# Expert stage: the second product's accumulators put two to a PSUM bank, four banks in rotation

## Chip, core and metric

One core of a Trainium2 chip runs the whole program. Its engines are TensorE (PE in the rows; PEld is its weight load), VectorE (DVE), ScalarE (ACT), GpSimd (POOL) and SyncE (SP, which issues most DMAs). The metric is the device time of one execution, in microseconds (us). PSUM, in which TensorE accumulates, has eight banks of 512 float32 columns over 128 partitions; this kernel uses all eight in the stage that is changed.

## What is computed

Three layers, one after the other. An FFT convolution over 8 x 3072 tokens of 256 features gives `x`. Then a mixture of eight experts, of which each token goes to one; then a dense two-product layer. The change is in the experts:

```
for e in range(E):                     # E = 8, FF = 1024, D = 256
    mask = e_idx == e                  # e_idx = argmax(x @ w_gate)
    ...
    h = np.maximum(x[mask] @ w1[e], 0.0)
    ye = h @ w2[e]
    out[mask] = gate_w[mask, None] * eom[mask, e, None] * ye
```

## The kernel before

The 24,576 tokens are grouped by expert into blocks: 41 blocks of 512 tokens and up to 21 of 256 tokens for what is left over (17 of them were executed). `experts(ids, first)` walks through the blocks; from the twelfth place on, a 256-token block stands after every two 512-token blocks. Each block takes eight ticks, one for each 128 of the 1024 hidden features. Numbers are split in a high and a low part (`hh` and `hl`, `w2h` and `w2l`), so each product is three matmuls: high with high, high with low, low with high.

A tick `t` records, in this order, which is also the order in which each engine executes (the schedule is written out by hand):

- TensorE: `gemm1` (L586), six matmuls of the first product into a bank of the pool `ph` (four banks).
- ScalarE: the relu (L867), which writes `hh`; then VectorE: the low part `hl` (L868).
- ScalarE and VectorE: one eighth of the next block's weights is split (`split_w`, L633 and L634). SyncE loads the weights of the block after that: `w1r` is issued in the fourth tick, `w2r` in the last (L613, L618), each 1 MB.
- TensorE: `gemm2` (L595) of the tick two before this one, into the block's accumulators `pz`. The accumulators collect over the block's eight ticks.
- Only after a block's last `gemm2`: ScalarE copies the accumulators out to `zo` (L896), and SyncE stores `zo` to HBM (L898).

A 512-token block has four accumulators of 128 tokens x 256 features, a 256-token block has two. Each has a bank of its own, of which it uses half. The four banks are named:

```
pz[j2] = pz_tiles(nt, 0 if nt == 4 or j2 % 2 else 2)
```

A 512-token block takes banks 0 to 3, a 256-token block 0 and 1 or 2 and 3 in turn. So the first `gemm2` of the next block goes into a bank that the block before has just finished with, and it must wait for that bank's copy. The two ticks between `gemm1` and `gemm2` mean that TensorE has one more `gemm1` to do after a block's last `gemm2`, before it comes to that wait.

The second layer (L923 on) has accumulators of the same kind (L1087, evicted at L1096) that already stand two to a bank.

Of the kernel before, what the change touches and what calls it, by code (L numbers as in the profile page):

```python
# [9 lines left out]
F32 = mybir.dt.float32  # L10
# [6 lines left out]
PSUM = bass.MemoryType.PSUM  # L17
# [3 lines left out]
NB, SEQ, D = 8, 3072, 256  # L21
# [105 lines left out]
def fftconv_moe_moe2(ctx: ExitStack, tc: tile.TileContext, x, ffl, fny, wg, w1, w2, win, wout,  # L127
                     t_sq, t_m2, t_m3, t_sg, t_sm, out):
    nc = tc.nc
    V, S, G, T = nc.vector, nc.scalar, nc.gpsimd, nc.tensor  # L130
# [145 lines left out]
    pools = {}  # L276
# [111 lines left out]
    def scatter(m, after=None):  # L388

        for i in range(min(m, len(scat))):  # L390
            b, n, pos, tid = scat.pop(0)
            if after is not None:
                G.tensor_copy(gap, after)
            else:
                G.memset(gap, 0.0)
            i = G.indirect_dma_start(
                out=xid, out_offset=bass.IndirectOffsetOnAxis(ap=pos[:, n:n + 1].bitcast(U32), axis=0),
                in_=tid[:, n:n + 1], in_offset=None)
            tc.declare_no_dep(i.ins, group="scatter", reason="every token has a row of its own")
            tc.add_to_no_dep_group("scatter", i.ins)  # L400
            if b >= BE:
                tc.declare_no_dep(i.ins, group="early", reason="the first blocks hold tokens of earlier batches")
                tc.add_to_no_dep_group("late", i.ins)
# [143 lines left out]
    pzs = ctx.enter_context(ExitStack())  # L547
# [32 lines left out]
    def gemm1(wh, wl, xh, xl, f, w):  # L580
        p = pools["ph"].tile([128, 512], F32, name="ph", tag="ph")
        n = 0
        for k in range(2):
            ws = slice(128 * f, 128 * f + 128)
            for a, b in ((wh, xh), (wh, xl), (wl, xh)):
                T.matmul(p[:, 0:w], a[:, k, ws], b[:, k, 0:w], start=n == 0, stop=n == 5)  # L586
                n += 1
        return p

    def gemm2(hh, hl, wh, wl, f, last, pz):  # L590
        for c, z in enumerate(pz):
            ts = slice(128 * c, 128 * c + 128)
            n = 0
            for a, b in ((hh, wh), (hh, wl), (hl, wh)):
                T.matmul(z, a[:, ts], b[:, f, :], start=f == 0 and n == 0, stop=f == last and n == 2)  # L595
                n += 1

    def pz_tiles(nt, first):
        return [pools["pz"].tile([128, 512], F32, name="pz", tag=f"pz{first + c}")[:, 0:D] for c in range(nt)]

    raw, wt, xg, xt = {}, {}, {}, {}

    def nt_of(j):
        return 4 if j < NFULL else 2

    def load_w(j, which):
        if j is None:
            return
        if which == 0:
            e = nc.sync.value_load(eidx[0:1, j:j + 1], min_val=0, max_val=E - 1)  # L610
            raw[j] = [e, None, None]
            t = pools["raw"].tile([128, 2, FF], F32, name="w1r")
            nc.sync.dma_start(t, w1[bass.ds(e, 1)].rearrange("o (c p) f -> p (o c) f", p=128))  # L613
            raw[j][1] = t
        else:
            e = raw[j][0]
            t = pools["raw"].tile([128, 8, D], F32, name="w2r")
            nc.sync.dma_start(t, w2[bass.ds(e, 1)].rearrange("o (c p) f -> p (o c) f", p=128))  # L618
            raw[j][2] = t

    def split_w(j, i):
        if j is None:
            return
        if i == 0:
            wt[j] = [pools["we"].tile([128, 2, FF], F32R, name="w1h"), pools["we"].tile([128, 2, FF], F32R, name="w1l"),
                     pools["we"].tile([128, 8, D], F32R, name="w2h"), pools["we"].tile([128, 8, D], F32R, name="w2l")]
        if i < 4:
            at = (slice(None), i // 2, slice(512 * (i % 2), 512 * (i % 2) + 512))
            src, h, l = raw[j][1][at], wt[j][0][at], wt[j][1][at]
        else:  # L630
            at = (slice(None), slice(2 * (i - 4), 2 * (i - 4) + 2), slice(None))
            src, h, l = raw[j][2][at], wt[j][2][at], wt[j][3][at]
        S.copy(h, src)  # L633
        V.tensor_tensor(l, src, h.bitcast(F32), op=ALU.subtract)  # L634
# [6 lines left out]
    def load_tok(j):  # L641
        if j is None:
            return
        nt = nt_of(j)
        assert j < NE or not (scat or gating)
        G.memset(gap, 0.0)
        ids = pools["m"].tile([128, 4], I32, name="ids")
        if nt == 4:
            i = G.indirect_dma_start(
                out=ids, out_offset=None, in_=xid.rearrange("(a c) o -> a (c o)", c=4),  # L650
                in_offset=bass.IndirectOffsetOnAxis(ap=xidx[:, j:j + 1].bitcast(U32), axis=0))
            early(j, i)
        else:
            for c in range(2):
                o = NFULL + 2 * (j - NFULL) + c
                G.indirect_dma_start(
                    out=ids[:, c:c + 1], out_offset=None, in_=xid,
                    in_offset=bass.IndirectOffsetOnAxis(ap=xidx[:, o:o + 1].bitcast(U32), axis=0))
        t = pools["m"].tile([128, 4, D], F32, name="xg")
        for c in range(nt):  # L660
            i = G.indirect_dma_start(  # L661
                out=t[:, c, :], out_offset=None, in_=yn if j >= NE else yn[0:BE * SEQ, :],
                in_offset=bass.IndirectOffsetOnAxis(ap=ids[:, c:c + 1].bitcast(U32), axis=0))
            early(j, i)
        xg[j] = t
# [130 lines left out]
    for k in range(ng * NB + 4 + nu):  # L796
        b, i = divmod(k, ng)
# [42 lines left out]
    load_w(1, 0)  # L840
    load_w(1, 1)
    latep.close()
    pools["pz"] = pzs.enter_context(tc.tile_pool(name="pzp", bufs=1, space=PSUM, side="right", reuse_waits="tile"))
    gating.append(gate(NB - 1, pools["ph"], "ph"))
    gating.append(tables())
    def clear():
# [7 lines left out]
    def experts(ids, first):  # L854
        ex = None
        hq, pz = {}, {}
        ns = 8 * len(ids)
        ids = ids + [None, None]
        for t in range(ns + 2):
            n, f = divmod(t, 8)  # L860
            j, ja, jb = (ids + [None])[n:n + 3]
            if t < ns:
                w = 128 * nt_of(j)
                p = gemm1(wt[j][0], wt[j][1], *xt[j], f, w)
                hh = pools["m"].tile([128, 512], F32R, name="hh", bufs=3)
                hl = pools["m"].tile([128, 512], F32R, name="hl", bufs=3)
                S.activation(hh[:, 0:w], p[:, 0:w], AF.Relu)  # L867
                V.scalar_tensor_tensor(hl[:, 0:w], p[:, 0:w], 0.0, hh[:, 0:w].bitcast(F32),  # L868
                                       op0=ALU.max, op1=ALU.subtract)
                hq[t] = hh, hl  # L870
                split_w(ja, f)
                if f == 3:
                    load_w(jb, 0)
                if f == 7:
                    load_w(jb, 1)
                if f == 4:
                    load_tok(jb)
                scatter(1, tick(hh[:, 0:1].bitcast(F32)))
                go_on(1)
                if first and ex is None and not gating and not scat:  # L880
                    open_layer_pools()
                    clear()
                    ex = extra()
                if ex is not None and j < NFULL:
                    next(ex, None)
            if t >= 2:
                j2, f2 = ids[(t - 2) // 8], (t - 2) % 8
                nt = nt_of(j2)
                if f2 == 0:
                    pz[j2] = pz_tiles(nt, 0 if nt == 4 or j2 % 2 else 2)  # L890
                hh, hl = hq.pop(t - 2)
                gemm2(hh, hl, wt[j2][2], wt[j2][3], f2, 7, pz[j2])
                if f2 == 7:
                    zo = pools["m"].tile([128, 4, D], F32, name="zo")
                    for c, z in enumerate(pz.pop(j2)):
                        S.copy(zo[:, c, :], z)  # L896
                    r0 = 512 * j2 if nt == 4 else ZREM + 256 * (j2 - NFULL)
                    nc.sync.dma_start(zs[r0:r0 + 128 * nt, :].rearrange("(p c) d -> p c d", c=nt), zo[:, 0:nt, :])  # L898
                    wt.pop(j2)
                    xt.pop(j2)  # L900
            if t < ns and f in (5, 6):
                prep_x(ja, f - 5)
# [23 lines left out]
    with ExitStack() as c3:  # L926
# [112 lines left out]
        hq, zq, zo, cc = {}, {}, {}, {}  # L1039
# [4 lines left out]
        def bank():  # L1044
            return pools["ph"].tile([128, 512], F32, name="ph", tag="ph")
# [79 lines left out]
        for t in range(npair + 1):  # L1125
# [17 lines left out]
            if j == 0:  # L1143
                ws = wsums(q)
                for n, u in enumerate(PLAIN):
# [3 lines left out]
                    b = bank()  # L1149
# [97 lines left out]
```

## Time and profile before

| | |
|---|---|
| time, median of 3 runs | 3904.09 us (3898.43 to 3909.12) |
| the profiled execution | 3879.73 us, its span 3878.0 us |
| TensorE busy | 3786.5 us, 98% of the span |
| VectorE, ScalarE, GpSimd busy | 70%, 61%, 26% |
| expert stage | from about 560 to 1760 us of the span |
| ScalarE's copies of 256 columns (L896) | 198, mean 387 ns |
| second layer's copies of 512 columns (L1096) | 96, mean 594 ns |

A row of a timeline gives the start and the duration in us, the engine, the line of the kernel, the operation, what it writes and reads, and in square brackets how long the engine had been idle and who ended that. A duration of a matmul is longer than its distance to the next one, since matmuls are pipelined. The granted clock is the share of TensorE's full clock: 1.00 is 2.4 GHz and 0.50 is 1.2 GHz.

### The profile page before, as it was taken

Reading aid. Unit: us, or ns where it says so; the run is one execution under the profiler, and the core shown is the slowest. Engines: PE = TensorE matmul, PEld = TensorE weight load, DVE = VectorE, ACT = ScalarE, POOL = GpSimd, SP = SyncE. Lnnn points to the kernel's source line nnn. Section 1 sums busy time; section 2 is a strip of 40 time slices with the busy share of each in tenths; the row PEclk is TensorE's granted clock in tenths of the full one; section 3 lists DMA queues with packets and bytes.
Section 4 is the critical chain, followed back from the end, with each engine's and each line's share of the span. In section 5 each row is a group of like instructions: output and inputs, shape, how many; then the busy total and the mean of one; then the engine's idle time right before and its main releaser. Section 6 shows DMA issues by size and latency. Waiting matters only on the chain.

```text
span 3878.0 us, 63612 instructions
## 1 busy us (share of the span) xinstructions
PE 3786.5 (98%) x24340; PEld 3378.1 (87%) x24340; DVE 2716.8 (70%) x4910; ACT 2378.2 (61%) x4573; POOL 1010.4 (26%) x1159
## 2 busy tenths in 40 slices
PE   6999999999999999998999999999999999999999
PEld 3777778898889899997899999999999999999998
DVE  4667766577878755555777777777777777777776
ACT  3777764455454555554666666666666666666666
POOL 3044556422222222215222111112222111112200
PEclk8999999999999999999999999999999999999999
DMA  9666543445555444440000000000000000000000
GB/s 253 207 204 200 171 147 121 145 137 173 167 164 163 161 159 148 154 138 28 28 25 25 34 22 23 23 23 27 23 26 25 33 23 23 23 23 27 24 17 22
DMA packets 195396, 345.09 MB, mean 89 GB/s; under 512 B 26320, under 2 KB 112464, under 8 KB 194704
## 3 DMA queue, kind: packets, MB, share of 16 engines
q1 hardware_dynamic: 167376, 289.60, 22.9%
q0 software_dynamic: 27296, 51.36, 4.8%
q8 instruction: 192, 3.15, 0.3%
q14 instruction: 116, 0.95, 0.1%
q10 hardware_dynamic: 416, 0.03, 0.0%
HBM read 238.31 MB, written 102.60 MB: 88 GB/s over the span
## 4 chain that ended last, share of the span: by engine, by line
PE 47%; ACT 4%; DVE 2%; issue 1%; POOL 0%; DMA 0%; ACTq 0%; POOLq 0%; DVEq 0%
PE pz L1087 23%; PE ph L1029 21%; ACT sig L1053 1%; PE ph L1035 1%; ACT zo L1096 1%; PE pt L958 1%; ACT sp L1066 1%; DVE cc L1204 1%; DVE xl L965 0%; ACT xh L964 0%; DVE cc L1193 0%; DVE rw L1001 0%; DVE hl L1062 0%; ACT hh L1058 0%; POOL zg L942 0%
## 5 line engine op out<-in xcount | busy, mean ns | idle before, releaser
L1087 PE MATMUL pz<-wouth,hh 128*128 128x256 f32 x3072 | 873.0, 284 | 0.0
L1087 PE MATMUL pz<-wouth,hl 128*128 128x256 f32 x3072 | 868.7, 283 | 0.0
L1087 PE MATMUL pz<-woutl,hh 128*128 128x256 f32 x3072 | 868.2, 283 | 0.0
L1062 DVE TENSOR_TENSOR hl<-cc,hh 128x512 fp32r<-128x512 f32 x768 | 523.3, 705 | 155.0 <-ACT hh L1058 154.3
L1087 PEld LDWEIGHTS pz<-wouth,hh 128*128 128x128 f32 x3072 | 585.3, 191 | 30.0
L1087 PEld LDWEIGHTS pz<-woutl,hh 128*128 128x128 f32 x3072 | 586.0, 191 | 26.8
L942 POOL DMA_INDIRECT zg<-zs,posz x192 | 213.2, 1111 | 1515.0 <-PE pt L958 1358.2
L1087 PEld LDWEIGHTS pz<-wouth,hl 128*128 128x128 f32 x3072 | 585.5, 191 | 0.3 <-DVE hl L1062 0.3
L867 ACT ACTIVATE hh<-ph 128x512 fp32r<-128x512 f32 (+1 forms) x464 | 249.0, 537 | 527.3 <-PE ph L586 440.4
L1066 ACT COPY sp<-ph 128x512 f32<-128x512 f32 x552 | 324.1, 587 | 381.4 <-PE ph L1029 380.4
L868 DVE SCALAR_TENSOR_TENSOR hl<-ph,hh 128x512 fp32r<-128x512 f32 (+1 forms) x464 | 283.6, 611 | 333.9 <-ACT hh L867 314.4
L1058 ACT CAST hh<-cc 128x512 fp32r<-128x512 f32 x768 | 476.1, 620 | 34.8 <-DVE cc L1161 33.0
L595 PE MATMUL pz<-w2h,hh 128*128 128x256 f32 x1584 | 447.9, 283 | 24.6 <-ACT zo L896 24.4
L595 PE MATMUL pz<-w2h,hl 128*128 128x256 f32 x1584 | 445.6, 281 | 0.0
L595 PE MATMUL pz<-w2l,hh 128*128 128x256 f32 x1584 | 445.2, 281 | 0.0
L1053 ACT ACTIVATE sig<-cc 128x512 f32<-128x512 f32 x552 | 349.4, 633 | 133.1 <-DVE cc L1204 67.9
L661 POOL DMA_INDIRECT xg<-yn,ids x198 | 199.5, 1008 | 758.7 <-PE ph L571 663.9
L586 PE MATMUL ph<-xh,w1h 128*128 128x512 f32 (+1 forms) x928 | 348.7, 376 | 4.1 <-issue 4.1
L586 PE MATMUL ph<-xl,w1h 128*128 128x512 f32 (+1 forms) x928 | 339.0, 365 | 0.3 <-DVE xl L577 0.2
L595 PEld LDWEIGHTS pz<-w2h,hh 128*128 128x128 f32 x1584 | 300.6, 190 | 43.5 <-ACT zo L896 29.2
L586 PE MATMUL ph<-xh,w1l 128*128 128x512 f32 (+1 forms) x928 | 335.7, 362 | 0.0
L595 PEld LDWEIGHTS pz<-w2l,hh 128*128 128x128 f32 x1584 | 302.1, 191 | 12.7
(240 smaller groups left out, 8280.6 us busy)
## 6 DMA issues: line engine op xcount, KB each, us to landing
w1r<-in_w_dram SPq DMA_DIRECT2D x58, 1024.0 KB
w2r<-in_w_dram SPq DMA_DIRECT2D x58, 1024.0 KB
us<-u SPq DMA_DIRECT2D x96, 256.0 KB
u<-us SPq DMA_DIRECT2D x128, 192.0 KB
out_dram<-zo SPq DMA_DIRECT2D x46, 512.0 KB
yn<-yt SPq DMA_DIRECT2D x90, 256.0 KB
xt<-in_x_dram SPq DMA_DIRECT2D x84, 256.0 KB
zs<-zo SPq DMA_DIRECT2D x41, 512.0 KB
```

Of the source, the lines that this page charges most:

```text
L586: T.matmul(p[:, 0:w], a[:, k, ws], b[:, k, 0:w], start=n == 0, stop=n == 5)
L595: T.matmul(z, a[:, ts], b[:, f, :], start=f == 0 and n == 0, stop=f == last and n == 2)
L661: i = G.indirect_dma_start(out=t[:, c, :], out_offset=None, in_=yn if j >= NE else yn[0:BE * SEQ, :], in_offset=bass.IndirectOffsetOnAxis( ...
L867: S.activation(hh[:, 0:w], p[:, 0:w], AF.Relu)
L868: V.scalar_tensor_tensor(hl[:, 0:w], p[:, 0:w], 0.0, hh[:, 0:w].bitcast(F32), op0=ALU.max, op1=ALU.subtract)
L942: G.indirect_dma_start(out=t[:, c, :], out_offset=None, in_=zs, in_offset=bass.IndirectOffsetOnAxis(ap=posz[0][:, o:o + 1].bitcast(U32), a ...
L1029: T.matmul(out, w, x, start=start and n == 0, stop=n == 2, skip_group_check=True)
L1053: S.activation(t, src, AF.Sigmoid, scale=1.702)
L1058: S.copy(hq[t, u][0], cc[u])
L1062: V.tensor_tensor(l, cc[u], h.bitcast(F32), op=ALU.subtract)
L1066: S.copy(t, x)
L1087: T.matmul(z[:, 256 * (c % 2):256 * (c % 2) + 256], a[:, ts], wm[w][:, 2 * q + i, :], start=first and m == 0, stop=m == 2, skip_group_chec ...
```

## The change

The accumulators become tiles of 2 x 256 columns, so that two share a bank: a 512-token block has two tiles, a 256-token block one. All tiles have one tag in a pool of four buffers, so the four banks are taken in turn, whatever the block's size. Only the first matmul into a bank carries the flag `start` (f = 0, first half); the second half's first matmul goes without it. A copy takes the whole bank, 512 columns.

```diff
-    def gemm2(hh, hl, wh, wl, f, last, pz):
-        for c, z in enumerate(pz):
-            ts = slice(128 * c, 128 * c + 128)
-            n = 0
-            for a, b in ((hh, wh), (hh, wl), (hl, wh)):
-                T.matmul(z, a[:, ts], b[:, f, :], start=f == 0 and n == 0, stop=f == last and n == 2)
-                n += 1
-
-    def pz_tiles(nt, first):
-        return [pools["pz"].tile([128, 512], F32, name="pz", tag=f"pz{first + c}")[:, 0:D] for c in range(nt)]
+    def gemm2(hh, hl, wh, wl, f, pz):
+
+        for b, z in enumerate(pz):
+            for c in range(2):
+                ts = slice(256 * b + 128 * c, 256 * b + 128 * c + 128)
+                for n, (a, w) in enumerate(((hh, wh), (hh, wl), (hl, wh))):
+                    T.matmul(z[:, c, :], a[:, ts], w[:, f, :], start=f == 0 and c == 0 and n == 0, stop=n == 2,
+                             skip_group_check=True)
+
+    def pz_tiles(nt):
+        return [pools["pz"].tile([128, 2, D], F32, name="pz", tag="pz") for _ in range(nt // 2)]
...
-    pools["pz"] = pzs.enter_context(tc.tile_pool(name="pzp", bufs=1, space=PSUM, side="right", reuse_waits="tile"))
+    pools["pz"] = pzs.enter_context(tc.tile_pool(name="pzp", bufs=4, space=PSUM, side="right", reuse_waits="tile"))
...
-                    pz[j2] = pz_tiles(nt, 0 if nt == 4 or j2 % 2 else 2)
+                    pz[j2] = pz_tiles(nt)
...
-                gemm2(hh, hl, wt[j2][2], wt[j2][3], f2, 7, pz[j2])
+                gemm2(hh, hl, wt[j2][2], wt[j2][3], f2, pz[j2])
...
-                        S.copy(zo[:, c, :], z)
+                        S.copy(zo[:, 2 * c:2 * c + 2, :], z)
```

No engine's instructions come in another order; what changes is the banks, the waits and the copies. TensorE at the first `gemm2` tick of the second block, before, with the engines that a row waits for in brackets (`Activation` is ScalarE):

```order
L595 MATMUL pz<-w2h,hh 128x256 [waits Activation_49]
L595 MATMUL pz<-w2l,hh 128x256
L595 MATMUL pz<-w2h,hl 128x256 [waits DVE_49]
L595 MATMUL pz<-w2h,hh 128x256 [waits Activation_49]
L595 MATMUL pz<-w2l,hh 128x256
L595 MATMUL pz<-w2h,hl 128x256
L595 MATMUL pz<-w2h,hh 128x256 [waits Activation_49]
L595 MATMUL pz<-w2l,hh 128x256
L595 MATMUL pz<-w2h,hl 128x256
```

The same nine places in the changed kernel, whose `gemm2` matmuls have line 596:

```order
L596 MATMUL pz<-w2h,hh 128x256 [waits Activation_49]
L596 MATMUL pz<-w2l,hh 128x256
L596 MATMUL pz<-w2h,hl 128x256 [waits DVE_49]
L596 MATMUL pz<-w2h,hh 128x256
L596 MATMUL pz<-w2l,hh 128x256
L596 MATMUL pz<-w2h,hl 128x256
L596 MATMUL pz<-w2h,hh 128x256
L596 MATMUL pz<-w2l,hh 128x256
L596 MATMUL pz<-w2h,hl 128x256
```

Before, each accumulator's first matmul waits for a copy of the block before; after, the one wait for ScalarE that is left is the one for this tick's `hh`. ScalarE at the end of a 512-token block, before:

```order
L867 ACTIVATE hh<-ph 128x512
L633 CAST w1h<-w1r 128x512
L896 COPY zo<-pz 128x256 x4
L867 ACTIVATE hh<-ph 128x512
L633 CAST w1h<-w1r 128x512
```

And at the same place in the changed kernel, where the relu is L868, the cast L634 and the copy L897:

```order
L868 ACTIVATE hh<-ph 128x512
L634 CAST w1h<-w1r 128x512
L897 COPY zo<-pz 128x512 x2
L868 ACTIVATE hh<-ph 128x512
L634 CAST w1h<-w1r 128x512
```

Four copies became two at the same place; on both sides they stand behind the relu and the weight cast of the next block's second tick.

## Rows read from the trace of the kernel before

**Rows 1.** The profile's page: the span, and each engine's busy time.

```profile
span 3878.0 us, 63612 instructions
PE 3786.5 (98%) x24340; PEld 3378.1 (87%) x24340; DVE 2716.8 (70%) x4910; ACT 2378.2 (61%) x4573; POOL 1010.4 (26%) x1159
```

**Rows 2.** Waits of TensorE in the expert stage (total, times, longest), and the page's group.

```profile
PE pz L595 <- ACT zo L896: 24.4, 13, 3.0
...
L595 PE MATMUL pz<-w2h,hh 128*128 128x256 f32 x1584 | 447.9, 283 | 24.6 <-ACT zo L896 24.4
```

**Rows 3.** Stretches: busy time by engine, granted clock, DMA share, GB/s.

```profile
1340.00:1700.00 360.00, 360.00 (x2492) 333.90 (x2491) 209.52 (x359) 187.72 (x392) 93.18 (x103) 1.00 0.47 154
2000.00:3800.00 1800.00, 1794.54 (x11722) 1633.21 (x11721) 1327.45 (x2046) 1197.60 (x2129) 362.27 (x320) 1.00 0.08 25
```

**Rows 4.** Timeline of one wait, where a 256-token block follows a 512-token block.

```profile
893.76 0.39 SPq L618 DMA_DIRECT2D w2r<-in_w_dram  x1
...
895.54 0.28 PE L586 MATMUL ph<-xh,w1l 128*128 128x256 f32 x1
...
897.68 0.28 PE L586 MATMUL ph<-xh,w1l 128*128 128x256 f32 x1
898.31 0.38 ACT L867 ACTIVATE hh<-ph 128x256 fp32r<-128x256 f32 x1 [3.69 <-PE ph L586]
...
898.73 0.42 DVE L868 SCALAR_TENSOR_TENSOR hl<-ph,hh 128x256 fp32r<-128x256 f32 x1 [2.94 <-ACT hh L867]
899.10 1.20 ACT L896 COPY zo<-pz 128x256 f32<-128x256 f32 x4
...
900.07 0.39 PE L595 MATMUL pz<-w2h,hh 128*128 128x256 f32 x1 [2.12 <-ACT zo L896]
...
900.62 0.42 DVE L868 SCALAR_TENSOR_TENSOR hl<-ph,hh 128x256 fp32r<-128x256 f32 x1 [0.69 <-ACT hh L867]
...
901.84 0.28 PE L595 MATMUL pz<-w2h,hl 128*128 128x256 f32 x1
...
903.26 0.28 PE L595 MATMUL pz<-w2h,hl 128*128 128x256 f32 x1
```

**Rows 5.** The stretch of that wait: busy time by engine, granted clock, DMA share, GB/s.

```profile
896.00:899.00 3.00, 1.96 (x17) 1.75 (x15) 0.27 (x1) 0.69 (x2) 1.56 (x2) 1.00 1.03 352
```

**Rows 6.** Timeline of TensorE: four of the thirteen waits.

```profile
593.36 0.39 PE L595 MATMUL pz<-w2h,hh 128*128 128x256 f32 x1 [1.47 <-ACT zo L896]
...
644.27 0.58 PE L595 MATMUL pz<-w2h,hh 128*128 128x256 f32 x1 [3.03 <-ACT zo L896]
...
1263.54 0.39 PE L595 MATMUL pz<-w2h,hh 128*128 128x256 f32 x1 [2.11 <-ACT zo L896]
...
1325.10 0.39 PE L595 MATMUL pz<-w2h,hh 128*128 128x256 f32 x1 [1.55 <-ACT zo L896]
```

**Rows 7.** TensorE alone in the five half-clock stretches: busy time, clock, DMA.

```profile
643.47:650.29 6.82, 6.02 (x22) 0.50 0.21 79
...
1264.69:1268.11 3.42, 3.42 (x18) 0.50 0.35 144
sum 20.48, PE 19.68; mean PE 3.94
```

**Rows 8.** ScalarE's copies out of accumulators by shape: busy, mean ns, idle before.

```profile
L896 ACT COPY zo<-pz 128x256 f32<-128x256 f32 x198 | 61.2, 387 | 5.5 <-PE ph L586 3.0 <-PE pz L595 2.4
...
L1096 ACT COPY zo<-pz 128x512 f32<-128x512 f32 x96 | 49.4, 594 | 3.7 <-PE pz L1087 3.3
```

**Rows 9.** Timeline: first and last of twelve accumulating matmuls, expert stage and second layer.

```profile
895.66 0.28 PE L595 MATMUL pz<-w2h,hh 128*128 128x256 f32 x1
...
896.96 0.28 PE L595 MATMUL pz<-w2h,hl 128*128 128x256 f32 x1
...
2406.90 0.28 PE L1087 MATMUL pz<-wouth,hh 128*128 128x256 f32 x1
...
2408.21 0.28 PE L1087 MATMUL pz<-wouth,hl 128*128 128x256 f32 x1
```

## The prediction

> **What bounds the kernel now.** I read the page first. TensorE is busy for 3786.5 of 3878.0 us [rows 1], so an edit in the expert stage can only gain what TensorE idles there, or what makes it slow there. The second view is therefore the waits of TensorE between 560 and 1760 us. One row holds nearly all: 24.4 us in 13 waits, the longest 3.0 us, of `gemm2` for ScalarE's copies out of `pz`; the page has the same sum on the first of the three matmuls of a `gemm2` [rows 2]. In a stretch of the stage after the last of these waits, TensorE works 360.00 of 360.00 us at full clock [rows 3]: no second limit shows behind TensorE, neither in ScalarE (188 us of 360) nor in VectorE (210).
>
> The third view is the timeline around one wait [rows 4], a 512-token block followed by one of 256. `gemm1` of the new block's second tick ends at 895.54 + 0.28 = 895.82. Its relu starts only at 898.31, 2.5 us late, and the copies stand behind that relu and a weight cast in ScalarE's order, so they start at 899.10. TensorE has meanwhile done one more `gemm1`, is through at 897.68 + 0.28 = 897.96, and stands for 2.12 us until the copy of its bank is done. The reader should see two things: ScalarE is late, not slow (it was idle for 3.69 us before that relu), and the copies pass this lateness on to TensorE. In those 3 us the DMA engines are fully occupied, share 1.03 at 352 GB/s [rows 5], by the 1 MB of `w2r` issued at 893.76 [rows 4]. That the load delays the signal from TensorE to ScalarE is a guess of mine; the change leaves it as it is.
>
> The fourth view is the granted clock. Five waits are followed by a stretch at 0.50, 1.2 GHz: the one that ends at 644.27 by 643.47 to 650.29, the one that ends at 1263.54 by 1264.69 to 1268.11 [rows 6, 7]. The five last 20.48 us together, with 19.68 us of TensorE work [rows 7]. Between 1340 and 1700 us, where there is no wait, the clock stays at 1.00 [rows 3].
>
> **The change part by part.** *The waits for the copies go.* A block's accumulators now lie in banks that the block before does not use; the last user of a bank is four tiles back, at least one whole 512-token block. The built order shows this: the waits for a copy at the first `gemm2` tick are gone, and the wait left on that tick's first matmul is for its own relu. Gain: 24.4 us [rows 2].
>
> *Half-clock stretches go with them.* Work of 19.68 us at 1.2 GHz is 9.84 us of work at 2.4 GHz, so 19.68 - 9.84 = 9.8 us come back if all five are due to the waits [rows 7]. From below it is nothing, if the clock falls there anyway; I take the whole, because the clock is at 1.00 in the 360 us without a wait.
>
> *What is late next.* The late relu stays, so its next reader is TensorE's `gemm2` of the same tick. In the timeline the low part `hl` of that tick is ready at 898.73 + 0.42 = 899.15, and the matmul that reads it runs at 901.84. Without the wait it would run 2.12 us earlier, at 899.72: still 0.57 us of slack. The following tick is tighter, since its relu stands behind the copies: `hl` is ready at 900.62 + 0.42 = 901.04, and its reader moves from 903.26 to 901.14. That leaves 0.10 us [rows 4]. So the cover is just enough at its tightest place. If it is missed by as much as it now holds, each of 13 places loses some 0.1 us, 1.3 us in all; I take 1 us. If the cover did not exist at all, the wait would only move from the copy to the relu, and 24.4 us would be the price.
>
> *Copies of 512 columns.* Four copies of 256 take 1.20 us together [rows 4]; two of 512, at 594 ns each by the second layer's [rows 8], take 1.19 us end to end and less where they overlap, as the four do (4 x 387 ns would be 1.55). The relu behind them is not later than now. At the stage's end the last block's copy is one of 594 instead of two of 387, of which the first overlaps matmuls: it lands about 594 - 387 = 0.2 us later, once, on the path to the second layer. VectorE, GpSimd and the DMA queues keep their instructions and order; their cover is TensorE, which stays the longest.
>
> *Two accumulators in one bank.* The order of matmuls stays; only the address changes. Twelve matmuls of the expert stage start 896.96 - 895.66 = 1.30 us apart, 118.2 ns from one to the next; twelve of the second layer, whose accumulators already share banks, 2408.21 - 2406.90 = 1.31 us, 119.1 ns [rows 9]. The 3 x 1584 = 4752 matmuls [rows 2] times 0.9 ns would cost 4.3 us. Whether the sharing makes this difference the trace cannot say, as the layers differ in operands too. The bounds are 0, as no row has a shared bank at a shorter distance, and some 12 us (2.5 ns each: both ends of the twelve read wrong by the last digit, 0.01 us, and the difference doubled to be safe); I take 0, since 0.01 us over eleven steps is all that the rows differ by.
>
> *Rotating through banks.* Both pools of the second layer rotate, and its clock is 1.00 over 1800 us with 1794.54 us of work [rows 3]: rotating does not lower the clock there. The Trainium skill, "TensorE: Matmul & The Clock Gate", section "A second HAM failure mode: psum-queue depth-cycling", tells of a kernel that cycles through PSUM banks each iteration, idles a little between groups, and loses throughput to a clock that swings between its two levels. By that rule the rotation could add half-clock stretches instead of taking five away; by the rows it takes them away. The rule has a place among the rivals.
>
> **Sum.** 24.4 + 9.8 - 1 - 0.2 = 33 us. TensorE is the long engine from there to the end (1794.54 of 1800 us [rows 3]), so the second layer starts and ends that much earlier. Against the profiled execution: 3879.7 - 33 = 3847. The median of the runs shown is 3904.1, 24.4 us above the profiled execution, and nothing shows where those 24.4 us lie; I take the same gain off it: **3871 us**. If they are more waits of the same kind, the gain is larger, up to 3904.1 - 33 - 24.4 = 3847.
>
> **Rivals.**
> *A. The waits come back in part at the relu.* For it: only 0.10 us of slack at the tightest place [rows 4], and a relu that is now late by 2.5 us could be later elsewhere. Against it: where the next tick is met, the copies take no longer than before. With half of the 34 us given back, 3904 - 17 = 3887.
> *B. Shared banks slow the matmuls by 2.5 ns.* Gain 33 - 12 = 21, 3883. For it the 0.9 ns of rows 9, against it that this is their reading error.
> *C. All of the wait moves to the relu, no change, 3904.* It needs ScalarE to be the pace of the stage; its 188 us in 360 [rows 3] speak against that.
> *D. Slower, by shared banks alone.* Place: all 4752 `gemm2` matmuls. It decides from 33 us / 4752 = 7 ns each, 125 ns apart instead of 118. At 130 ns, 12 more than now, it costs 57 us: 3904 - 33 + 57 = 3928. The second layer's 119.1 ns [rows 9] speak against it.
> *E. Slower, by a swinging clock.* If each of the 58 blocks brought a stretch as that of 3.42 us, half lost [rows 7], 99 us would be added, the five of now (9.8) included: 3904 - 24 + 99 - 10 = 3969; it decides from about 20 blocks. This is the skill's rule above; rows 3 speak against it.
>
> **How the numbers follow.** The full gain, 28 to 38 us on the median (3866 to 3876), has a chance of 0.66; A 0.10, B 0.10, C 0.09, D 0.03, E 0.02. A measurement of this kernel can tell about 0.3%, 12 us, from no change. Faster by more than that: 0.66 + 0.10 + 0.10 = 0.86; within it 0.09; slower 0.05. The range takes in A and B upward, and downward the case that the unexplained 24.4 us hold more of these waits: 3847 to 3888. C to E, 0.14, lie outside. The likeliest case alone has 3866 to 3876.
>
> **What would show it.** In the profile after, TensorE's waits in the expert stage should have no row for `zo`; its busy time there should reach its length, with a granted clock of 1.00 between 600 and the stage's end. The stage should end some 33 us earlier and the second layer keep its length. A row of TensorE waiting for `hh` or `hl` would show rival A or C; starts of `gemm2` more than 120 ns apart B or D; half-clock stretches at block starts E. There should be 99 copies of about 590 ns. The prediction is wrong if the slack at the second tick after a boundary is not there: 0.10 us was read at one place.

## The result, and the profile after

The changed kernel takes 3856.02 us, median of 6 runs (3851.9 to 3864.79). The kernel before took 3905.44 us beside it (6 runs, 3898.43 to 3912.71), so the ratio is 0.9885 with an interval of 0.987 to 0.99: faster by 49 us. The prediction was 3871, with a range of 3847 to 3888: the time lies in the range, but below the 3866 to 3876 that it held likeliest.

The profiled execution took 3853.38 us, 26.4 us less than that of before (3879.73), where the prediction's sum has 33. In the changed kernel `gemm2` is L596, the relu L868, `hl` L869 and the copy L897. First its page: the span, the busy time of the engines, and the groups of two of the three `gemm2` matmuls; rows of before are [rows 1, 2].

```profile
span 3851.6 us, 63513 instructions
PE 3778.9 (98%) x24340; PEld 3370.9 (88%) x24340; DVE 2709.8 (70%) x4910; ACT 2369.3 (62%) x4474; POOL 1016.6 (26%) x1159
...
L596 PE MATMUL pz<-w2h,hh 128*128 128x256 f32 x1584 | 445.3, 281 | 0.1
L596 PE MATMUL pz<-w2l,hh 128*128 128x256 f32 x1584 | 443.6, 280 | 0.3 <-issue 0.3
```

The group that held 24.6 us of idle time before it [rows 2] now holds 0.1 us. TensorE's waits between 540 and 1760 us (total, times, longest):

```profile
PE pt L959 <- DVE zg L953: 9.6, 4, 7.4
PE pt L959 <- DVE xl L966: 3.6, 2, 2.2
PE ph L586 <- DVE xl L577: 2.4, 3, 1.6
PE pa L312 <- ACT gh L299: 1.1, 2, 0.7
PE pz L596 <- DVE hl L869: 1.1, 1, 1.1
PE pz L596 <- issue: 0.8, 2, 0.5
```

There is no row for `zo`. The first two rows belong to the second layer, behind the expert stage. The stretches (busy time in the order PE, PEld, DVE, ACT, POOL, then granted clock, DMA share, GB/s); the first one runs between two half-clock stretches, the second from the start of the first `gemm1` of the expert stage to the end of its last `gemm1`:

```profile
541.50:1732.76 1191.26, 1182.60 (x8038) 1084.60 (x8036) 821.91 (x1753) 608.71 (x1232) 362.78 (x438) 1.00 0.48 156
...
563.31:1727.88 1164.57, 1160.00 (x7917) 1068.51 (x7917) 811.06 (x1711) 590.23 (x1185) 346.84 (x420) 1.00 0.48 156
...
2000.00:3800.00 1800.00, 1794.72 (x11720) 1633.05 (x11719) 1325.50 (x2043) 1196.00 (x2125) 352.89 (x312) 1.00 0.07 25
```

The clock is 1.00 over 1191 us in one piece, where five half-clock stretches lay before [rows 7]. The same stage of the kernel before, with a sixth half-clock stretch that the prediction did not list; it lies in the first block, ahead of any copy:

```profile
558.14:564.96 6.82, 4.33 (x10) 2.60 (x10) 2.34 (x5) 2.02 (x4) 2.46 (x5) 0.50 0.71 210
...
557.14:1752.89 1195.75, 1168.35 (x7916) 1075.73 (x7917) 818.14 (x1710) 599.02 (x1283) 344.36 (x421) 0.99 0.47 152
```

So the stage went from 1195.75 to 1164.57 us, 31.2 us shorter, and the second layer works as before (1794.72 against 1794.54 of 1800 us [rows 3]). In a second trace of the changed kernel (`after_again`, below) the stage took 6 us more, so that 25.2 us are gained:

```profile
559.73:1730.23 1170.50, 1162.75 (x7917) 1069.33 (x7917) 810.36 (x1711) 589.73 (x1185) 341.75 (x420) 1.00 0.48 155
```

The part ahead of the stage, which the change does not touch, was 6.2 us longer in the first of these executions (563.31 against 557.14).

Now the boundary that rows 4 show, in the changed kernel: the same two blocks, TensorE, ScalarE and VectorE.

```profile
882.66 0.39 SPq L619 DMA_DIRECT2D w2r<-in_w_dram  x1
...
884.45 0.28 PE L586 MATMUL ph<-xh,w1l 128*128 128x256 f32 x1
884.56 0.28 PE L596 MATMUL pz<-w2h,hh 128*128 128x256 f32 x1
...
885.86 0.28 PE L596 MATMUL pz<-w2h,hl 128*128 128x256 f32 x1
...
888.03 0.38 ACT L868 ACTIVATE hh<-ph 128x256 fp32r<-128x256 f32 x1 [4.51 <-PE ph L586]
888.10 0.28 PE L586 MATMUL ph<-xh,w1l 128*128 128x256 f32 x1
...
888.45 0.43 DVE L869 SCALAR_TENSOR_TENSOR hl<-ph,hh 128x256 fp32r<-128x256 f32 x1 [3.75 <-ACT hh L868]
...
888.47 0.38 PE L596 MATMUL pz<-w2h,hh 128*128 128x256 f32 x1
...
888.82 1.08 ACT L897 COPY zo<-pz 128x512 f32<-128x512 f32 x2
...
888.93 0.38 PE L596 MATMUL pz<-w2h,hl 128*128 128x256 f32 x1
...
891.98 0.28 PE L596 MATMUL pz<-w2h,hh 128*128 128x256 f32 x1
```

Four things stand in these rows. The relu is still late: its `gemm1` ends at 884.45 + 0.28 = 884.73 and it starts at 888.03, 3.3 us later (2.5 before). The copies at 888.82 stop nobody. The relu's own reader stands for it now: `gemm1` at 888.10, the next matmul 0.37 us later instead of 0.12, and its third matmul 0.46 us behind the first instead of 0.24. And twelve matmuls of one block start 885.86 - 884.56 = 1.30 us apart, as before [rows 9].

The packed traces also hold the times at which TensorE raised the semaphore for which the relu waits. In the changed kernel they have none between 882.61 and 888.01, while matmuls go on starting, and then five within 0.4 us; in the kernel before they have none between 893.70 and 898.29. The relu starts 0.02 us after that rise in both. So it is TensorE's signal that is late, as the prediction guessed, and ScalarE follows it at once. Whether the matmuls themselves ended late the traces cannot tell, since their ends are modelled; what delays the signal stays open (below).

### The profile page after: what moved, and what is told of

Its sections match the earlier page's. It is cut to its first block, busy times and chain, and to the rows that moved or that the text cites. A ratio compares the mean times of both kernels' runs of the same rounds, so it can differ in the third digit from the quotient of the medians.

```text
span 3851.6 us, 63513 instructions
## 1 busy us (share of the span) xinstructions
PE 3778.9 (98%) x24340; PEld 3370.9 (88%) x24340; DVE 2709.8 (70%) x4910; ACT 2369.3 (62%) x4474; POOL 1016.6 (26%) x1159
## 4 chain that ended last, share of the span: by engine, by line
PE 48%; ACT 4%; DVE 3%; issue 1%; POOL 0%; DMA 0%; ACTq 0%; DVEq 0%; POOLq 0%
PE pz L1088 24%; PE ph L1030 22%; ACT sig L1054 1%; ACT zo L1097 1%; PE pt L959 1%; PE ph L1036 1%; ACT sp L1067 1%; DVE cc L1205 1%; DVE xl L966 0%; ACT xh L965 0%; DVE cc L1194 0%; DVE rw L1002 0%; DVE hl L1063 0%; ACT hh L1059 0%; DVE cc L1191 0%
## 5 line engine op out<-in xcount | busy, mean ns | idle before, releaser
L868 ACT ACTIVATE hh<-ph 128x512 fp32r<-128x512 f32 (+1 forms) x464 | 249.9, 539 | 492.9 <-PE ph L586 439.1
L869 DVE SCALAR_TENSOR_TENSOR hl<-ph,hh 128x512 fp32r<-128x512 f32 (+1 forms) x464 | 283.5, 611 | 316.2 <-ACT hh L868 300.1
L596 PE MATMUL pz<-w2h,hl 128*128 128x256 f32 x1584 | 445.6, 281 | 1.6 <-DVE hl L869 1.1
L596 PE MATMUL pz<-w2h,hh 128*128 128x256 f32 x1584 | 445.3, 281 | 0.1
L596 PE MATMUL pz<-w2l,hh 128*128 128x256 f32 x1584 | 443.6, 280 | 0.3 <-issue 0.3
L596 PEld LDWEIGHTS pz<-w2h,hh 128*128 128x128 f32 x1584 | 298.7, 189 | 15.8 <-ACT hh L868 0.8
L596 PEld LDWEIGHTS pz<-w2l,hh 128*128 128x128 f32 x1584 | 300.2, 190 | 12.7
```

The lines of the kernel that those rows point to most:

```text
L596: T.matmul(z[:, c, :], a[:, ts], w[:, f, :], start=f == 0 and c == 0 and n == 0, stop=n == 2, skip_group_check=True)
```

## The experiments

In three of the five sets of runs the kernel before took 3837 us and not 3904: the program is the same, the chip is another (the record has chips 8 and 10 at 3837, chip 1 at 3904, and no number for the first set, at 3904). That it is the chip, and not something else that differs between sets of runs, is not shown. The expectations were written without knowing which chip would come. I call the chips by these times, the 3904 chip and the 3837 chips (two different ones).

### Is the gain there on every chip: before, two banks, four copies, no load

`before_again`, the unchanged kernel of before, run once:

> The kernel before, unchanged, for a second trace: its timed runs have a median of 3905 us, its first trace a span of 3878. Theory (all of the gain is waits for the copies and the half-clock stretches behind them): a trace with a span near 3900 has more than 24.4 us of these waits, and waits plus half of the half-clock time in the expert stage come to about 50 us or more, against 34 in the first trace. Rival (the missing 24 us lie outside the expert stage, in the convolution or the second layer): waits near 24 us again, and the convolution or the second layer longer by some 20 us.

`two_banks` shares the banks and copies 512 columns, but does not rotate far enough:

```diff
-    pools["pz"] = pzs.enter_context(tc.tile_pool(name="pzp", bufs=4, space=PSUM, side="right", reuse_waits="tile"))
+    pools["pz"] = pzs.enter_context(tc.tile_pool(name="pzp", bufs=2, space=PSUM, side="right", reuse_waits="tile"))
```

> The changed kernel with two buffers in place of four: accumulators still two to a bank and copied out in 512 columns, but the next 512-token block needs the same two banks. Theory (the gain is the rotation's): the waits for the copies come back, 25 to 50 us, ratio to the kernel before 0.995 to 1.003. Rival (fewer, larger copies relieve ScalarE, or the shared bank helps TensorE): ratio near 0.9885, with few waits.

`four_copies` is the changed kernel with copies of 256 columns:

```diff
-                        S.copy(zo[:, 2 * c:2 * c + 2, :], z)
+                        for h in range(2):
+                            S.copy(zo[:, 2 * c + h, :], z[:, h, :])
```

> The changed kernel with each bank copied out in two copies of 256 columns, as before the change; banks shared and rotating over four. Theory (the size of the copy is nothing): ratio to the kernel before 0.987 to 0.990 as the changed kernel, no waits of TensorE for copies, the waits for hl at most 1 to 3 us. Rival (half of the gain came from the larger copies): ratio near 0.994, with waits for hh or hl.

`no_w2_load` is the kernel before without the load that the prediction suspected, from the ninth block on:

```diff
-            t = pools["raw"].tile([128, 8, D], F32, name="w2r")
-            nc.sync.dma_start(t, w2[bass.ds(e, 1)].rearrange("o (c p) f -> p (o c) f", p=128))
-            raw[j][2] = t
+            if j < NE:
+                t = pools["raw"].tile([128, 8, D], F32, name="w2r")
+                nc.sync.dma_start(t, w2[bass.ds(e, 1)].rearrange("o (c p) f -> p (o c) f", p=128))
+                kept.append(t)
+            raw[j][2] = kept[-1]
```

> The kernel before, with the 1 MB load of w2r left out from the ninth 512-token block on and in all 256-token blocks: they split the second-product weights that lie in the buffer, so those blocks compute with another expert's second weights. Theory (the load makes ScalarE learn late of TensorE's work, and that lateness makes the waits): from about 800 us on the waits for the copies go, the ones before 726 us stay; ratio 0.989 to 0.993. Rival (ScalarE is late at a block's start whatever the load, through its own order of work): the eight waits of 1.5 to 2.1 us between 900 and 1326 us stay, ratio 0.998 to 1.002.

Measured, against 3836.81 us of before on that chip (27 runs): `before_again` 3836.21 us; `two_banks` 0.9998 (0.9989 to 1.0007); `four_copies` 1.0001 (0.9992 to 1.001); `no_w2_load` 1.0003 (0.9993 to 1.0012). None of the differences that were expected came, since what they were to divide was not there. A later trace of the unchanged kernel on the other 3837 chip (`before_third`, below) shows why; its stage, its waits between 530 and 1760 us, and the boundary of rows 4:

```profile
558.55:1713.55 1155.00, 1153.24 (x7917) 1066.53 (x7917) 820.83 (x1711) 599.30 (x1283) 346.15 (x426) 1.00 0.49 157
```

```profile
PE pt L958 <- DVE zg L952: 9.9, 4, 7.7
PE pt L958 <- DVE xl L965: 3.4, 2, 1.9
PE pz L595 <- DVE hl L868: 0.9, 1, 0.9
```

```profile
874.76 0.39 SPq L618 DMA_DIRECT2D w2r<-in_w_dram  x1
...
876.54 0.28 PE L586 MATMUL ph<-xh,w1l 128*128 128x256 f32 x1
876.66 0.28 PE L595 MATMUL pz<-w2h,hh 128*128 128x256 f32 x1
...
876.86 0.38 ACT L867 ACTIVATE hh<-ph 128x256 fp32r<-128x256 f32 x1 [1.24 <-PE ph L586]
...
877.65 1.20 ACT L896 COPY zo<-pz 128x256 f32<-128x256 f32 x4
...
883.07 0.28 PE L595 MATMUL pz<-w2h,hh 128*128 128x256 f32 x1
```

The relu starts at 876.86, 0.04 us after its `gemm1` ends (876.54 + 0.28), where it was 2.5 us late on the 3904 chip; TensorE's semaphore rises at 876.84. The copies start 0.83 us after that end (877.65), where they came 3.28 us after it on the 3904 chip (899.10 against 895.82 [rows 4]). TensorE waits for none of them, and the stage takes 1155.00 us. Where ScalarE is not late, the kernel before has no wait for the change to take. The changed kernel itself did not run on these chips; its variants did, and gained nothing.

That makes these runs a price list of the other parts. `four_copies` has shared banks and rotation, `two_banks` shared banks and large copies; their upper ends, 1.001 and 1.0007, are 3.8 and 2.7 us over 4752 `gemm2` matmuls, 0.8 and 0.6 ns each. Sharing a bank does not cost the 2.5 ns of rival B. The traces say it more sharply: from the first `gemm2` at the boundary shown to the end of the stage's last `gemm1`, `before_third` and `four_copies` take the same time, and TensorE is busy in all of it. The 3.9 us by which the whole stage of `four_copies` is longer lie in its first block, ahead of any copy.

```profile
876.66:1713.55 836.89, 836.89 (x5838) 778.95 (x5837) 592.52 (x1175) 440.62 (x925) 200.55 (x230) 1.00 0.50 161
```

```profile
876.40:1713.29 836.89, 836.89 (x5838) 779.39 (x5837) 592.90 (x1175) 441.73 (x925) 200.54 (x230) 1.00 0.50 161
```

### Making ScalarE late on purpose

On a 3904 chip (before there 3903.49 us, 13 runs) ScalarE got extra work ahead of the relu of every block's second tick, in the kernel before (`before_late`), in the changed one (`after_late`) and in the one with two banks (`two_banks_late`). The extra copies write a tile that nobody reads; they took 2.44 us (four of 512 columns) and 3.19 us (eight of 256), more than the 2.0 to 2.2 of the expectation:

```diff
+                if f == 1:
+                    late = pools["m"].tile([128, 512], F32, name="late", bufs=1)
+                    for _ in range(4 if w == 512 else 8):
+                        S.copy(late[:, 0:w], p[:, 0:w])
                 S.activation(hh[:, 0:w], p[:, 0:w], AF.Relu)
```

> The kernel before, with ScalarE made late at each block's start: in the second tick it first copies that tick's fresh first product into a scratch tile, four times 512 or eight times 256 columns, some 2.0 to 2.2 us. Theory (on the chip of the prediction the relu of that tick came late, and the copies behind it; where it is not late the kernel before has no wait for the copies): on a chip where the kernel before takes some 3837 us, waits for the copies return, about 1.5 us at each of 17 changes to a 256-token block and 0.5 to 1 us at the others, 40 to 60 us, with half-clock stretches behind some; ratio 1.012 to 1.022. Rival (the two ticks between the products hide a late ScalarE, and the waits have another cause): ratio 0.999 to 1.003.

> The changed kernel with the same lateness of ScalarE. Theory (rotation takes the copies off TensorE's path, and the relu's lateness of about 2 us fits into the two ticks between the products): no wait for copies, waits for hh or hl of at most 5 us in all; against the kernel before without the lateness a ratio of 0.999 to 1.003 on a chip where that kernel takes 3837 us, 0.986 to 0.992 on one where it takes 3905. Rival (the wait only moves from the copies to the relu's low part): ratio as that of the kernel before with the lateness, 1.012 to 1.022.

> The changed kernel with two buffers in place of four, and the same lateness: banks shared, copies of 512 columns, no rotation over four. Theory (rotation alone takes the wait away): ratio 1.012 to 1.024, as the kernel before with the lateness. Rival (fewer copies are enough): ratio below 1.006.

> The changed kernel once more, beside the kernel before on the same chip. Theory (the gain is only there where ScalarE comes late): ratio 0.987 to 0.990 if the kernel before takes some 3905 us here, 0.998 to 1.002 if it takes some 3837. Rival (the change has a gain of its own): ratio 0.987 to 0.990 in both cases.

Measured: `before_late` 4040.78 us, 1.0345 (1.0327 to 1.0364); `two_banks_late` 4039.68 us, 1.0349 (1.0332 to 1.0367); `after_late` 3904.71 us, 1.0003 (0.9994 to 1.0013); `after_again` 3856.23 us, 0.9883 (0.9866 to 0.9899). TensorE's waits between 540 and 1930 us, first in `before_late`:

```profile
PE pz L595 <- ACT zo L900: 138.9, 56, 6.0
```

In `two_banks_late`:

```profile
PE pz L596 <- ACT zo L901: 145.0, 56, 6.0
```

In `after_late`:

```profile
PE pz L596 <- ACT hh L872: 28.0, 17, 3.2
```

This is the clearest pair of the study. With the same work added at each boundary, the kernel before pays 138.9 us of waits for the copies at 56 places, and the kernel that shares banks and has large copies but only two banks pays 145.0. With four banks there is no row for `zo`, and 136 us of the time are gone (4040.78 - 3904.71). `two_banks_late` and `after_late` differ in the number of banks alone, so the rotation takes the wait away; sharing a bank is only what makes room for it. And the wait does come back at the relu, as rival A has it, once ScalarE is late enough: 28.0 us at 17 places, with six half-clock stretches between 895 and 1343 us, of 27.31 us together:

```profile
895.45:902.28 6.83, 5.59 (x26) 5.59 (x27) 4.10 (x8) 5.10 (x14) 0.00 (x0) 0.50 0.29 86
...
sum 27.31, PE 25.07 PEld 25.07 DVE 19.22 ACT 22.07 POOL 0.00; mean PE 4.18 PEld 4.18 DVE 3.20 ACT 3.68 POOL 0.00
```

`after_late` is 48 us above `after_again`: the cover of the change is finite, and the lateness that it met by itself (3.3 us at the boundary shown) lay at its edge. Of the four expectations that of `after_again` was met. `before_late` (whose forecast was for a 3837 chip) and `two_banks_late` came out slower than forecast. `after_late`, for which 0.986 to 0.992 and at most 5 us of waits were expected on this chip, gave back the whole gain.

### What is still open: the untraced time, the load, the copies' place

`before_third` is the unchanged kernel again, for a trace of an ordinary execution on a 3904 chip:

> The unchanged kernel of before once more, for its trace. The profiled execution of before that the prediction rests on took 24.4 us less than the median of its runs. If this run takes some 3,905 us and the missing time is more of the same thing, its expert stage is longer than the 1195.8 us of that execution by about 20 us, with more than 24.4 us in TensorE's waits for the copies and more than five half-clock stretches there. The rival: the missing time lies ahead of the stage or in the second layer, and the stage is as long as it was. On a chip where the kernel takes some 3,837 us there should be no wait for a copy and no half-clock stretch, as in the run of before that was seen on such a chip, and the question stays open.

`no_w2_load_2` and `no_w2_load_3` repeat `no_w2_load`; in all three the load is left out from the ninth block on (NE is 8), which the first of these two texts names otherwise:

> The kernel of before without the 1 MB load of the second weights from the fifth-to-load block on: the blocks use the second weights already there, of another expert, so its output is another one. Repeats the run of the same kernel that fell on a chip where ScalarE is not late. On a chip where before takes some 3,905 us: if the load at the block boundary delays TensorE's signal, the relu of the second tick is late by well under the 2.5 us of rows 4, the waits for the copies fall below 10 us and the time by 25 to 45 us (0.989 to 0.993). If the load has no part in it, lateness, waits and time stay as they are (0.998 to 1.002). On a chip where before takes some 3,837 us: no difference, and nothing is learnt.

> The kernel of before once more without the 1 MB load of the second weights, from the ninth block on: these blocks use the second weights that already lie there, of another expert, so the output is another one. On a chip where before takes some 3,905 us: if the load at the block boundary delays TensorE's signal, the relu of the second tick is late by well under the 2.5 us of rows 4 from the ninth block on, the waits for the copies fall below 10 us and the time by 25 to 45 us (0.989 to 0.993). If the load has no part in it, lateness, waits and time stay as they are (0.998 to 1.002). On a chip where before takes some 3,837 us: no difference, and the guess stays open.

`late_evict` is the changed kernel with a block's copies behind the relu of the next block's third tick (the block's copies and store, put in a function `evict`, are called there):

```diff
                 S.activation(hh[:, 0:w], p[:, 0:w], AF.Relu)
+                if due:
+                    evict(due.pop(0))
...
                 if f2 == 7:
-                    zo = pools["m"].tile([128, 4, D], F32, name="zo")
...
+                    due.append(j2)
+                    if t >= ns:
+                        evict(due.pop(0))
```

> The changed kernel with a block's two copies put one tick later in ScalarE's order, behind the relu of the next block's third tick instead of ahead of it; with rotating banks nobody waits for them. Theory: on a chip where the changed kernel stands at 0.9885, what is left over there is about 1 us at each of eight boundaries, lost in three ticks after a late relu; the copies are 1.2 us of that lateness for the third tick and those after it, so about two of three lost parts go: 3 to 6 us less than the changed kernel, 0.987. The rival: the left-over comes from the late signal alone, which the order of the copies does not touch, and the time is that of the changed kernel, 0.988 to 0.989. On a chip where before takes some 3,837 us: no difference from before, 0.999 to 1.001.

All four came to a 3837 chip. Measured: `before_third` 3838.61 us; `no_w2_load_2` 1.0003 (0.9994 to 1.0012); `late_evict` 1.0006 (0.9997 to 1.0015); `no_w2_load_3` 0.9998 (0.9988 to 1.0007). So the questions that they were to answer stay open on the 3904 chip: whether the load has a part in the lateness was not seen there, nor whether later copies would give some microseconds more, and no execution of before with an ordinary time was traced there.

The traces at hand speak against the load as the cause by itself. Of the kernel before on the 3904 chip, two boundaries of the same kind as that of rows 4, the first earlier and the second later in the stage:

```profile
835.32 0.37 SPq L618 DMA_DIRECT2D w2r<-in_w_dram  x1
...
837.28 0.28 PE L586 MATMUL ph<-xh,w1l 128*128 128x256 f32 x1
837.91 0.39 ACT L867 ACTIVATE hh<-ph 128x256 fp32r<-128x256 f32 x1 [1.55 <-PE pz L595]
...
1379.25 0.37 SPq L618 DMA_DIRECT2D w2r<-in_w_dram  x1
...
1381.21 0.28 PE L586 MATMUL ph<-xh,w1l 128*128 128x256 f32 x1
1381.82 0.38 ACT L867 ACTIVATE hh<-ph 128x256 fp32r<-128x256 f32 x1 [1.53 <-PE pz L595]
```

```profile
1382.00:1385.00 3.00, 3.00 (x26) 2.84 (x25) 1.12 (x2) 1.99 (x7) 1.95 (x2) 1.00 1.04 362
```

The same load is issued 2.2 us ahead of the end of the `gemm1` (2.1 in rows 4), and in the second case the DMA engines are then as full (1.04, 362 GB/s) as in rows 5. Yet these relus start at most 0.35 us after the `gemm1` ends (837.56 to 837.91 and 1381.49 to 1381.82), and TensorE does not stop. The load alone does not make the signal late. What I can say is where the late boundaries lie: the eight from 893 to 1325 us lie all between the first and the last load of the second layer's weights, which go on beside the experts in that time:

```profile
871.23 0.79 SPq L692 DMA_DIRECT2D cvr<-in_win_dram  x1
...
1338.31 0.35 SPq L692 DMA_DIRECT2D cvr<-in_wout_dram  x1
```

That is a coincidence in time and no shown cause, since the 3837 chips have the same loads and no late relu there, and five of the thirteen waits (593 to 724 us) lie ahead of the first of these loads.

## Why the prediction was right, and where its sizes were off

*The waits for the copies go, 24.4 us.* Right: no row for `zo` in either trace of the changed kernel, and with added lateness 138.9 us against none.

*The half-clock stretches go with them, 9.8 us.* Right: five behind the waits before, none after over 1191 us, in either trace. The three late kernels show the same from the other side: where the waits are back, at the copy or at the relu, the clock falls again (0.96 over the stage in `before_late` and `two_banks_late`, six stretches in `after_late`). Not every wait brings one: five of thirteen did before. What the prediction made of the Trainium skill as rival E ("TensorE: Matmul & The Clock Gate", section "A second HAM failure mode: psum-queue depth-cycling") did not come: with four banks in turn the clock stays at 1.00. That does not contradict the section, whose kernel also idles between groups of matmuls; here that idling is what went (1160.00 of 1164.57 us busy).

*The residual at the late relu, 1 us.* Mis-sized. The reference for it is the kernel before on a chip where no relu is late at a block boundary: 1155.00 us of stage against 1164.57, so 9.6 us are left after the change (15.5 in the second trace). At the boundary shown, from the first `gemm2` of a block's last tick to that of the next block's fourth, 6.41 us pass without lateness (876.66 to 883.07), 7.42 after (884.56 to 891.98), 8.79 before (895.66 [rows 9] to the row below). One microsecond is lost at such a place and not 0.1.

```profile
904.45 0.28 PE L595 MATMUL pz<-w2h,hh 128*128 128x256 f32 x1
```

The step that failed is the slack: it took the lateness as fixed, 2.5 us, and found 0.57 us for the first reader. In the changed kernel the relu was 3.3 us late, so the slack was used up and each of three ticks lost some 0.3 us. At a boundary of the same trace where the lateness stayed at 2.5 us (1120.93 to 1123.45) the slack nearly held: the same distance is 6.64 us (1120.77 to 1127.41), 0.2 us lost and not 1.0:

```profile
1120.65 0.28 PE L586 MATMUL ph<-xh,w1l 128*128 128x256 f32 x1
1120.77 0.28 PE L596 MATMUL pz<-w2h,hh 128*128 128x256 f32 x1
...
1123.45 0.39 ACT L868 ACTIVATE hh<-ph 128x256 fp32r<-128x256 f32 x1 [3.72 <-PE ph L586]
...
1127.41 0.28 PE L596 MATMUL pz<-w2h,hh 128*128 128x256 f32 x1
```

Six of the eight late boundaries lost about 1 us in this trace, and all eight did in the second one; at each of these the relu was 3.2 to 3.3 us late. Why the signal came later than in the kernel before is not known. The rest of the 9.6 us, some 3, lies ahead of the boundary shown (321.25 us from the stage's start against 318.11). Rival A was thus at work, in a small way, and the prediction's own sign of being wrong, a slack that is not there, came true in this term. The waits' view shows nearly nothing of it, since a gap of 0.2 or 0.3 us between matmuls lies within their own 0.28 us.

The same blindness worked on the other side, too. The stage before lost 1195.75 - 1155.00 = 40.8 us, of which the waits and stretches in the sum are 34.2. Of the 6.6 us between, 2.8 lie in the first block, with the sixth half-clock stretch and ahead of any copy (27.60 us to the second block's first `gemm1`, against 24.83); the other 3.8 are in no row of that view. So the gain of the stage, 31.2 us (25.2 in the second trace), came out near the 33 of the sum by luck, as two errors offset each other: 40.8 less 9.6 (or 15.5), where the prediction had 34.2 less 1.2.

*The median.* The step that was off by most. The profiled execution of before was 24.4 us below its median, and the prediction took the same 33 us off the median. Measured were 49.4 us, above the 28 to 38 to which it gave 0.66. The time is in the range by the downward case alone, that the 24.4 us hold more of these waits, to which it gave no chance of its own. The two traces of the changed kernel lie 2.6 and 1.4 us below their medians, those of `before_late` and `two_banks_late` 1.6 and 4.0 us above theirs, so a traced execution is not shorter as such: that one of before was an easy one. The granted clock of the untraced runs says a little on what it lacked: on the 3904 chip it was 0.986 to 0.990 for before (0.990 in the profile) and 0.992 to 0.994 for the changed kernel. Some 0.001 of a mean clock is 0.002 of the span at half clock, 8 us, of which half is lost: about 4 us, an estimate. Some of the rest may lie ahead of the stage: in the traces on the 3904 chip the stage starts at 557.14 us (`before`, the earliest) to 571.72 (`before_late`), with the same instructions ahead of it. Whether there were more waits of the same kind was not seen in a trace.

*Shared banks, rotation, large copies.* Right at nothing: 1.30 us for twelve matmuls, mean durations of 280 and 281 ns against 283 [rows 2], the ratios of `two_banks` and `four_copies`, and the 836.89 us of the latter. The 99 copies have a mean of 593 ns:

```profile
L897 ACT COPY zo<-pz 128x512 f32<-128x512 f32 x99 | 55.3, 593 | 18.2 <-PE pz L596 8.4 <-PE ph L586 8.2 <-remote 1.6
```

*The other rivals.* B and D fall with the distance between matmuls, E with the clock, C with the size of the waits for `hh`, which have no row in the changed kernel until ScalarE is made later still. One reading was wrong without a price: not always a whole 512-token block lies between two uses of a bank; the block behind a 256-token block takes a bank that was last used just before that one.

## What to carry to other kernels

Here a wait for an eviction was removed by distance; larger copies without it did not remove it (`two_banks_late`). Give the accumulator another bank than the one just finished, and make the banks free by packing two accumulators into one. Before promising the gain, ask why the evicting engine was late, and whether it is late on another chip; here the change is worth 1.2% where ScalarE's signal is late and its variants gained nothing where it is not. And sum lateness by distances between the same two instructions in two traces, for a waits' view leaves out gaps shorter than a matmul's own duration.

## What the runs showed of the hardware

- One program has two times in sets of runs on different chips: 3903 to 3905 us, and 3836 to 3837 us on two others, the runs of each within 0.4% of each other. Of the 41 us between the traces' spans (3878.0 and 3836.8), 40.8 lie in the expert stage (1195.75 against 1155.00 us); what makes the other 26 us between the medians was not traced.
- On the 3904 chip the relu behind a finished `gemm1` started 1.8 to 3.3 us late at the eight block boundaries between 880 and 1330 us, with ScalarE idle (4.51 us before the relu in the trace after), while TensorE went on. TensorE's semaphore rose that late and the relu 0.02 us behind it. On the 3837 chips the relu started 0.04 us after the same matmul's end at the same place, with the same load beside it. The cause was not found.
